# Score packs in two halves, gelu one batch at a time, and new planned durations in a fused attention and GEGLU block

## The chip, the cores and the metric

The kernel runs on one core of a Trainium2 chip. The time is device microseconds from start to end of one execution. Three runs of the kernel before gave a median of 789.99 us (789.24 to 791.8). The engines are TensorE (PE, matmuls), VectorE (DVE), ScalarE (ACT), GpSimd (POOL) and SyncE (SP, which issues most DMAs).

## The reference

One transformer block over 2048 positions of width 640, in bfloat16: layer norm, attention with 32 query heads of width 20 that share one key and one value head, a residual sum, layer norm, and a feed-forward of width 1536 with a gelu gate.

```python
q = (ln(x) @ wq)  # 32 heads of 20
k = ln(x) @ wk;  v = ln(x) @ wv          # one head of 20, shared
p = softmax(q k^T * 20 ** -0.5)
h = x + (p v) @ wo
out = h + (gelu(ln(h) @ w_gate) * (ln(h) @ w_up)) @ w_down
```

## The kernel before

**The work and its tiles.** The 2048 positions are 16 tiles of 128. Attention goes through them in chunks (`CHUNKS`): seven of two tiles and two of one tile, 14 and 15. A chunk is worked in units; a unit is 512 query columns for each of four row strips of the array, so there are 32 units. For each unit and each of 16 key tiles there is one *pack*: four score products of 32 rows by 512 columns, one in each row strip, into four PSUM banks (L1126). That is 512 packs, 2048 products. Each product is then exponentiated into SBUF and multiplied with the values (L1205), accumulating into bank 6 or 7.

**Two ways to the exponential.** ScalarE takes one bank (512 columns) or two adjacent ones (1024) in one activation (L1466). VectorE takes a bank by writing the exponential as a linear function of the bits (L1552); such a product needs two shifted copies, made by GpSimd (L1529, L1515) or VectorE (L1509), and so three value products instead of one. How many of a pack's four products go to VectorE (0, 1, 2, or 4) is decided in `issue_qk` from the planned loads of both engines, the length of the pending shifts, and `stall`, an estimate of ScalarE's wait for the next pack.

**Side products.** Between packs TensorE does everything else in pieces: queries, keys and values, the output projection (`wo_job`), and the feed-forward's gate, up and down products (`gate_job`, `up_job`, `down_job`), all through the helper at L529 (four column strips) while packs are left, or L525 (the whole array) at the end. The feed-forward runs in batches equal to the chunks: 0 to 6 of two tiles, 7 and 8 of one. A batch needs its chunk's attention, the projection and the second layer norm. Its gate products are copied to `gbuf` while exponentials are left (L843), and the gelu is then taken in place on ScalarE (L870); once no exponentials are left, the gelu reads PSUM directly (L845). Exponential and gelu need different activation tables, so each excursion costs a table load both ways. `MERGE` says which batches wait for each other before their gelu: (0,1), (2,3), (4,5), (6,7), (8). Up products follow a batch's gelu, down products its up products, and a later batch may write its part of `gbuf` only when the earlier batch in the same columns is down.

**Who sets the order.** The program holds its own planner. It simulates the five engines with a table of costs (`c_pe`, `c_act`, `c_dve`, L-constants) and picks for the engine that is free first what it does next: `pe_decide`, `act_decide`, `dve_decide`, `pool_decide`, `sp_decide`. `pe_decide` issues a pack when four banks are free, else a value round or a side product that fits before the next pack, else, if TensorE has been quiet, a fill. The result is a fixed list of instructions for each engine, with semaphore waits only where a dependency needs one. On the chip each engine goes through its list in order, as fast as the waits allow. The planner's durations thus set order, not time.

**Other names the change touches.** `LNT`: from this tile on, the second layer norm goes ahead of other VectorE work. `load`: the first DMAs, with the latency that the planner books for each. `xn2T`: the transposed input of the feed-forward; batch b uses columns from 512 times (b mod 2), and may be written when batch b-2 has done its up products. `SP2G`: the gain in ns above which a pack gives VectorE two products.

The condition for a pack, before:

```python
        ok, allb = free_banks(t)
        if cand and len(ok) >= 4:
            issue_qk(t, cand[0], cand[1], ok)
            return True
```

Of the kernel before, what the change touches and what calls it, by code (L numbers as in the profile page):

```python
# [5 lines left out]
BF16 = mybir.dt.bfloat16  # L6
# [3 lines left out]
P = 128  # L10
# [11 lines left out]
class _Op:  # L22
    __slots__ = ("eng", "fn", "deps", "t0", "end", "vis", "idx", "dma", "need", "count", "sem", "clock")

    def __init__(self, eng, fn, deps, t0, end, vis, dma):
        self.eng = eng
        self.fn = fn
        self.deps = deps
        self.t0 = t0
        self.end = end  # L30
        self.vis = vis
        self.dma = dma
        self.need = False
        self.count = 0
        self.sem = None
        self.clock = None


class _Plan:
# [60 lines left out]
    def resolve(self):  # L100
# [6 lines left out]
        while left:  # L107
            moved = False
            for e in self.ENGINES:
                while pos[e] < len(self.ops[e]):  # L110
# [34 lines left out]
                    moved = True  # L145
            assert moved, "the plan has a cycle"
        for e in self.ENGINES:
            n = 0
            for op in self.ops[e]:
                if op.need and not op.dma:  # L150
                    n += 1
                    op.count = n

    def emit(self, name, eng, sems):
        done = 0
        for op, waits in zip(self.ops[name], self.waits[name]):
            for d in waits:
                if d.dma:
                    eng.wait_ge(d.sem, 16)
# [45 lines left out]
def bass_sequential_preLN__grouped_kv_mqa__glu_gated_geglu__prompt_kernel(  # L205
# [29 lines left out]

    CHUNKS = [[0, 1], [2, 3], [4, 5], [6, 7], [8, 9], [10, 11], [12, 13], [14], [15]]
    BATCHES = CHUNKS
    BATCH_COL = [0, 256, 0, 256, 0, 256, 0, 256, 384]
    LN2G = CHUNKS
    MERGE = [(0, 1), (2, 3), (4, 5), (6, 7), (8,)]  # L240
    PE_T1 = (0, 1)
# [5 lines left out]
    ND = 8  # L247
    NQ = 4
    NXT = 4
    NON = 8  # L250
# [10 lines left out]
    xn1T = sb("xn1T", [P, NC_D, S], BF16)  # L261
    xn2T = sb("xn2T", [P, NC_D, 1024], BF16)
    wq_pad = sb("wq_pad", [P, NG, NC_D, P], BF16)
# [6 lines left out]
    wd_sb = sb("wd_sb", [P, NFC, D], BF16)  # L270
    qT = sb("qT", [P, NQ, 512], BF16)
    kT4 = sb("kT4", [P, S], BF16)
    v_ext = sb("v_ext", [P, NT, 3, 32], BF16)
# [6 lines left out]
    onT = sb("onT", [P, 4, NC_D, P], BF16)  # L280
    gbuf = sb("gbuf", [P, NFC, 512], BF16)
    ident = sb("ident", [P, P], BF16)
# [48 lines left out]
    SP2 = 1  # L331
    SP2D = 400.0
    SP2P = 3
    SP2G = 300.0
    ADD_MIN = 1
    PVF = 99
    QUIET = 0.5
    PADD_DVE = 1
    PADD_LEN = 2
    PRA = 3  # L340
# [6 lines left out]
    NP0 = 4  # L347
    LNT = 12
    SPK = 1
# [44 lines left out]
    sp_tasks = []  # L394
    state = {"mode": "m", "tab": "exp", "npack": 0, "exps_left": 2048, "misc_ready": False, "kv_left": NT, "qk_left": 512}
    bank_owner = {b: None for b in range(8)}
    slots = {"xt": list(range(NXT)), "q": list(range(NQ)), "onT": list(range(4)), "osb": [0, 1], "rcp": [0, 1], "onr": [0, 1]}
    pa_free = [True] * NA
# [25 lines left out]
    def ln_group(ln, tiles, prio, done):  # L424
# [27 lines left out]
        def norm(t):  # L452
# [9 lines left out]
            def then(op):  # L462
# [47 lines left out]
    for t in range(NT):  # L510
        on_before[t] = [x for x in range(t) if onslot[x] == onslot[t]]
    xcol = {}
    for b, tl in enumerate(BATCHES):
        for i, t in enumerate(tl):
            xcol[t] = (b % 2) * 512 + i * P

# [95 lines left out]
    def q_job(u):  # L612
# [10 lines left out]
        def then(b):  # L623
# [5 lines left out]
            flex_copy(qT[:, s, :], bank(b), 512, [("b", b)], [("q", s)], 0.6, fin)  # L629

        def gate():
            if u["q"] is None:
# [9 lines left out]
        jb = _Job(("q", u["id"]), 1.0, pieces, then, gate)  # L642
        jobs.append(jb)

# [146 lines left out]
    def g_free(b):  # L791
        if any(("wqp", g) not in plan.w for g in range(NG)):
            return False

        mine = set(gkeys(b, 0))
        return all(down_left[x] == 0 for x in range(b) if mine & set(gkeys(x, 0)))

# [248 lines left out]
    def stall(t, n, fb):  # L1046
# [20 lines left out]
        free.sort()  # L1067
        return max(0.0, free[3] + 460.0 - ta)

    def issue_qk(t, u, kt, fb):  # L1070
        A = max(act_end() - t, 0.0)
        Dv = dve_load(t)
        if state["tab"] == "gelu" or any(tk.engs[0] == "act" for tk in tasks):
            A += sum(tk.cost[1] for tk in tasks if tk.engs[0] == "act" and isinstance(tk.cost, tuple)) + 1300.0
        nf = pd_free.count(True) - len(dve_q)
        burst = A > 3000.0
        if state["npack"] < NP0:
            n = 0
        elif burst:
            n = 4 if Dv < 2500.0 else 2  # L1080
        elif Dv > TH0:
            n = 0
        elif Dv < TH2 or (SP2 and Dv < SP2D and len(pend[1]) + len(pend[2]) < 2 * SP2P
                          and stall(t, 1, fb) + 1382.0 - stall(t, 2, fb) - 956.0 > SP2G):
            n = 2
        else:
            n = 1
        n = max(0, min(n, nf))

        k = state["npack"]  # L1090
        rr = [(k + i) % 4 for i in range(4)]
        bk = {}
        tiles = {}
        want = (4 - n) // 2 if n != 2 or PAIR2 else 0
        fb = list(fb)
# [9 lines left out]
        fb.sort(key=lambda b: ((b ^ 1) in fb, b))  # L1105
        ns = 4 - n - 2 * len(units_a)
        dbanks = [fb.pop(0) for _ in range(n)]
# [30 lines left out]
        for e in al:  # L1138
            act_q.append(("S" if len(e) == 1 else "P", [tiles[r] for r, b in e]))
        u["npk"] += 1  # L1140
        u["left"].remove(kt)
        u["todo"] += 4 + 2 * n
        if not u["left"]:
            u["closed"] = True
            slots["q"].append(u["q"])
        state["npack"] += 1
        _DEBUG.setdefault("joblog", []).append((t, ("qk", u["id"])))
        state["qk_left"] -= 1
# [29 lines left out]
    def issue_pv(t, qs, k):  # L1178
# [69 lines left out]
    def pe_decide(t):  # L1248
        cand = next_pack(t)
        piece = next_piece(t)  # L1250
        state["misc_ready"] = piece is not None
        ok, allb = free_banks(t)
        if cand and len(ok) >= 4:
            issue_qk(t, cand[0], cand[1], ok)
            return True

        tq = 1e12
        if cand:
# [34 lines left out]
        swv = pe_sw(t, "v")  # L1293
        can_v = nr >= 1 and (fits(220.0 + swv) or press)
        can_m = piece is not None and fits(c_pe(piece[1][1], "v") + (
# [23 lines left out]
    def fill(t):  # L1319
# [13 lines left out]
        state["mode"] = "v"  # L1333
        plan.commit("pe", fn, 222.0 + sw, L_PE, ["zz"] + [("k", k) for k in range(4)], [("b", ab)], at=t)
        state["fills"] = state.get("fills", 0) + 1
        return True

    def next_piece(t):
# [26 lines left out]
        for jb in jobs:  # L1365
            pr = jb.prio
            if jb.name[0] == "q":
                ahead = jb.name[1] - cur
                pr = 0.2 if ahead <= 0 else (0.9 if ahead <= 1 else 8.0 + 0.01 * ahead)
            if best is not None and pr >= best[0]:  # L1370
                continue
# [19 lines left out]
    def issue_piece(t, jb, pc):  # L1391
        if isinstance(jb, _Start):
            b = jb.b
            jb = jb.jb
            jobs.remove(jb)
            active.append(jb)
            jb.bank = b
            bank_owner[b] = jb.name
            if jb.name[0] == "q":
                units[jb.name[1]]["q"] = slots["q"].pop(0)  # L1400
        b = jb.bank
        fn = pc[0]
# [133 lines left out]
    def dve_decide(t):  # L1536
# [54 lines left out]
        if n and pend[w][0]["at"] <= t + 20:  # L1591
# [3 lines left out]
            if n >= 4 or pd_free.count(True) < 3:  # L1595
                pr = 0.2
            if n >= (PADD_LEN if POOL_ADD else ADD_MIN):
                opts.append((pr, len(opts), None))
# [109 lines left out]
    sems = {e: sem("c_" + e) for e in plan.ENGINES}  # L1708
    n = 0
    for e in plan.ENGINES:  # L1710
        for op in plan.ops[e]:
            if op.dma:
                op.sem = sem("d%d" % n)
                n += 1
    outs = [op for op in plan.ops["sp"] if op.dma]

    with nc.Block() as block:

        @block.sync
        def _(e):  # L1720
            plan.emit("sp", e, sems)
            for op in outs[-NT:]:
                e.wait_ge(op.sem, 16)

# [48 lines left out]
```

## Time and profile before

| | us |
|---|---|
| median of 3 runs | 789.99 |
| the profiled execution, time | 789.72 |
| its span, first to last instruction | 787.5 |
| PE busy | 688.1 (87%) |
| ACT busy | 728.2 (92%) |
| DVE busy | 622.6 (79%) |
| POOL busy | 626.9 (80%) |

Rows of groups read: line, engine, operation, output from input with shapes, count, then busy us and mean ns of one, then idle time of the engine just before, with what ended it. Rows of the order of time read: start us, length us, what, count; one row may hold several instructions. Rows of windows read: from and to, length, busy us of the engines with the count of instructions in brackets, then the granted TensorE clock, the busy share of the DMA engines and GB/s. A wait row reads: who waited for whom, us in total, times, the longest. A record of an activation or a matmul is longer than the time until the next can start, so records on one engine overlap.

### The profile page before, as it was taken

To read this page: it belongs to the slowest core of one execution; us is meant where nothing else is said; L and a number is where in the kernel's file an instruction comes from. 1 tells how busy PE (TensorE), PEld (TensorE's weight loads), DVE (VectorE), ACT (ScalarE), POOL (GpSimd) and SP (SyncE) were. 2 spreads that over 40 slices of the span, in tenths; PEclk is the share of its full clock that TensorE was granted. 3 is DMA by queue.
4 is the path that set the end of the run, shared out by engine and by line. 5 is a ranking of instruction groups with operands and counts; after the bars stand their busy time and mean duration, and the time that the engine had idled before them with its cause. 6 is when DMAs were issued, how large, how long until landed. Compare 5 with 4: busy or idle time off the path is not lost.

```text
span 787.5 us, 28823 instructions
## 1 busy us (share of the span) xinstructions
PE 688.1 (87%) x12613; PEld 327.8 (42%) x12613; DVE 622.6 (79%) x1128; ACT 728.2 (92%) x1054; POOL 626.9 (80%) x683
## 2 busy tenths in 40 slices
PE   4878778887879899899789899999888889999898
PEld 3322223342334444455234444445233444444477
DVE  7768879878888777977897877877798877877752
ACT  5789999999999999999999999999999999999940
POOL 5579998789978888698978897798998879787810
PEclk9799999999999999999999999999999999999999
DMA  7690000100110002100210001100001010111000
GB/s 204 158 283 12 9 7 19 26 10 8 25 25 9 3 26 27 26 26 10 23 27 2 9 18 34 26 26 10 9 19 26 9 10 26 23 30 26 11 2 34
DMA packets 56604, 25.81 MB, mean 33 GB/s; under 512 B 47649, under 2 KB 55201, under 8 KB 56481
## 3 DMA queue, kind: packets, MB, share of 16 engines
q1 hardware_dynamic: 55168, 23.55, 13.1%
q8 instruction: 100, 1.64, 0.9%
q10 hardware_dynamic: 1312, 0.44, 0.2%
q14 instruction: 24, 0.19, 0.1%
HBM read 10.21 MB, written 2.62 MB: 16 GB/s over the span
## 4 chain that ended last, share of the span: by engine, by line
PE 49%; ACT 30%; DVE 15%; DMA 2%; issue 2%; POOL 2%; POOLq 0%
ACT pa L1466 28%; PE ps L529 18%; PE ps L1126 13%; PE ps L1205 13%; DVE pd L1552 9%; PE ps L525 4%; ACT gbuf L870 1%; DVE xn_tmp L491 1%; DVE osb L1232 1%; DMA onr<-osb 1%; POOL pd L1529 1%; DMA xn1T<-xn_tmp 1%; DVE pd L1509 1%; DMA onT<-onq 1%; DVE gbuf L887 1%
## 5 line engine op out<-in xcount | busy, mean ns | idle before, releaser
L1466 ACT ACTIVATE pa<-ps 128x1024 bf16<-128x1024 f32 (+1 forms) x1013 | 689.0, 836 | 21.1 <-PE ps L1126 15.8
L1529 POOL TENSOR_TENSOR pd<-pd,shifts 128x512 int32<-128x512 int32 x531 | 544.8, 1041 | 94.6 <-DVE pd L1552 88.5
L1552 DVE TENSOR_SCALAR pd<-ps 128x512 uint16<-128x512 f32 x608 | 408.4, 688 | 127.9 <-PE ps L1126 117.1
L1205 PE MATMUL ps<-pd,v_ext 128*32 128x512 bf16 x1824 | 279.8, 384 | 18.1 <-DVE osb L1232 10.2
L1205 PE MATMUL ps<-pa,v_ext 128*32 128x512 bf16 x1440 | 256.7, 385 | 3.1 <-ACT pa L1466 2.5
L1126 PE MATMUL ps<-qT,kT 32*128 32x512 bf16 x2048 | 203.7, 385 | 60.9 <-DVE pd L1552 34.7
L1126 PEld LDWEIGHTS ps<-qT,kT 32*128 32x128 bf16 x2048 | 58.6, 91 | 221.9 <-DVE pd L1552 124.2
L1205 PEld LDWEIGHTS ps<-pd,v_ext 128*32 128x32 bf16 x1824 | 76.8, 95 | 81.2 <-issue 34.7
L1205 PEld LDWEIGHTS ps<-pa,v_ext 128*32 128x32 bf16 x1440 | 68.3, 95 | 39.2 <-issue 24.2
L529 PE MATMUL ps<-xn2T,wg_sb 128*32 128x256 bf16 (+1 forms) x1828 | 68.5, 270 | 1.0 <-DVE gbuf L843 0.5
L529 PE MATMUL ps<-wd_sb,gbuf 128*32 128x320 bf16 x1152 | 57.7, 301 | 1.0 <-DVE gbuf L887 1.0
L529 PE MATMUL ps<-xn2T,wu_sb 128*32 128x256 bf16 x1440 | 58.1, 274 | 0.3 <-DVE gbuf L887 0.3
L529 PE MATMUL ps<-xn1T,wq_pad 128*32 128x256 bf16 (+1 forms) x1440 | 53.3, 272 | 0.5 <-ACT pa L1466 0.4
L529 PEld LDWEIGHTS ps<-xn2T,wg_sb 128*32 128x32 bf16 x1828 | 43.9, 96 | 20.6 <-issue 12.2
L529 PEld LDWEIGHTS ps<-xn2T,wu_sb 128*32 128x32 bf16 x1440 | 36.8, 96 | 16.3 <-issue 7.9
L1515 POOL TENSOR_TENSOR pd<-pd,shifts 128x256 int32<-128x256 int32 x63 | 41.6, 669 | 1.3 <-DVE pd L1552 1.3
L529 PEld LDWEIGHTS ps<-xn1T,wq_pad 128*32 128x32 bf16 x1440 | 34.5, 99 | 16.0 <-issue 8.4
L529 PEld LDWEIGHTS ps<-wd_sb,gbuf 128*32 128x32 bf16 x1152 | 29.0, 96 | 23.3 <-issue 11.1
L887 DVE TENSOR_TENSOR gbuf<-ps,gbuf 128x512 bf16<-128x512 f32 x48 | 32.7, 681 | 6.6 <-PE ps L525 6.1
L1509 DVE TENSOR_SCALAR pd<-pd 128x512 uint16<-128x512 uint16 (+1 forms) x70 | 36.5, 534 | 0.0
L421 DVE BATCH_NORM_STATS2 stats<-xh 128x6 f32<-128x320 bf16 x64 | 29.8, 476 | 1.2 <-DMA xh<-in_A_x_dram 1.0
L529 PE MATMUL ps<-wo_sb,onT 128*32 128x320 bf16 x600 | 28.9, 301 | 1.3 <-DMA onT<-onq 0.7
(73 smaller groups left out, 363.2 us busy)
## 6 DMA issues: line engine op xcount, KB each, us to landing
out_dram<-xh SPq DMA_DIRECT2D x16, 160.0 KB, 1.8
xh<-in_A_x_dram SPq DMA_DIRECT2D x3, 640.0 KB, 8.0
wg_sb<-in_B_w_gate_dram SPq DMA_DIRECT2D x1, 1920.0 KB, 9.7
wu_sb<-in_B_w_up_dram SPq DMA_DIRECT2D x1, 1920.0 KB, 8.3
wd_sb<-in_B_w_down_dram SPq DMA_DIRECT2D x1, 1920.0 KB, 14.0
wo_sb<-in_A_wo_dram SPq DMA_DIRECT2D x1, 800.0 KB, 5.3
onr<-osb SPq DMA_TRANSPOSE x30, 2.4
gbuf<-in_A_wq_dram ACTq DMA_DIRECT2D x1, 400.0 KB, 4.9
```

Of the source, the lines that this page charges most:

```text
L421: dve(lambda e: e.bn_stats(stats[:, ln, t, 6 * h:6 * h + 6], xh[:, t, h * HALF:(h + 1) * HALF]), 395, [key], [("st", ln, t, h)], prio, c)
L491: tk.fn = lambda e: e.tensor_scalar(xn_tmp[:, s, :], xh[:, t, :], mv[:, ln, t, 0:1], ln_r[:, ln, t:t + 1], ALU.subtract, ALU.mult)
L525: return e.matmul(o(b), l, r, start=st, stop=sp)
L529: ins = e.matmul(o(b)[a, :], l[:, a], r, start=st, stop=sp, tile_position=(0, 32 * j))
L887: dve(lambda e: e.tensor_tensor(o, i, o, ALU.mult), c_dve(n * k), [("b", bk)] + ks, ks, 1.0, fin)
L1126: ins = e.matmul(bank(b), kT4[32 * r:32 * r + 32, kt * P:(kt + 1) * P], qT[32 * r:32 * r + 32, s, :], start=True, stop=True, tile_position ...
L1205: ins = e.matmul(ps[32 * r:32 * r + 32, ab * 512:(ab + 1) * 512], v_ext[:, it["kt"], it["w"], :], it["ap"], start=st, stop=(j in ends), ti ...
L1466: op = plan.commit("act", lambda e: e.activation(dst, src, ACT.Exp, scale=SM_SCALE), cost, L_ACT, [("b", b0 + i) for i in range(n)], [("pa ...
L1509: return e.tensor_scalar(pd[:, w, a], pd[:, 0, a], float(CH_SHIFT[w]), None, ALU.add)
L1515: return e.tensor_tensor(pd32[:, w, h], pd32[:, 0, h], shifts[:, w - 1:w].to_broadcast([P, 256 * k]), ALU.add)
L1529: return e.tensor_tensor(pd32[:, 1:3, h], pd32[:, 0, h].unsqueeze(1).to_broadcast([P, 2, 256]), shifts[:].unsqueeze(2).to_broadcast([P, 2, ...
L1552: op = plan.commit("dve", lambda e: e.tensor_scalar(pd[:, 0, s * 512:(s + 1) * 512], bank(b), CH_A, CH_B, ALU.mult, ALU.add), c_dve(512), ...
```

## The change

Several edits in the same program, which is planned anew with all of them:

- A pack may be issued in two halves of two products. When no four banks are free but two are, the side work at hand is at most `LIGHT` = 10 pieces, more than 20 packs are done, ScalarE's table is the exponential's, and ScalarE is planned to wait over 150 ns (`HGAIN`) if the whole pack were waited for, the first two rows are issued; the other two follow when two banks are free. Until then no other pack starts. A half gives VectorE one product if its load is under 1300 ns and fewer than three products wait for shifts, none otherwise (two while ScalarE is away for long).
- `MERGE` splits (4,5) and (6,7) into single batches.
- Planned durations: a side product costs n/2.4 + 3 ns in every mode (before n/2.4 + 9, at least 99, between packs), a value round 216 instead of 222; the value weights' load is booked with 4400 instead of 3000.
- `SP2G` 250 instead of 300; `stall` looks at the third free bank instead of the fourth when little side work is there; `LNT` 8 instead of 12.
- `xn2T` is a ring of four tiles (512 columns instead of 1024); batch 8 now lies beside batch 7 and follows batch 5's columns, not batch 6's. The columns of `gbuf` stay as they were.
- DMAs share semaphores in chains: a DMA joins a chain if the last of it is known to be done when it is issued, and its waiters wait for 16 times its place.
- A way to send queries through memory is added and off (`QD` = 99); `PH` with three equal values each changes nothing.

```diff
-    MERGE = [(0, 1), (2, 3), (4, 5), (6, 7), (8,)]
+    MERGE = [(0, 1), (2, 3), (4,), (5,), (6,), (7,), (8,)]
...
+    HALF_ON = 1
+    HGAIN = 150.0
+    HBEG = 20
+    SIX = 2
+    LIGHT = 10
+    HD0 = 1300.0
+    HP0 = 3
+    QD = 99
...
-        return max(n / 2.4, 54.0) + 3.0 if mode == "m" else max(n / 2.4, 90.0) + 9.0
+        return max(n / 2.4, 26.0) + 3.0
...
-    LNT = 12
+    LNT = 8
...
-    load("sp", wv_sb[:], cview(A_wv), ["wv"], 3000)
+    load("sp", wv_sb[:], cview(A_wv), ["wv"], 4400)
...
-                    return ln == 0 or batch_of[t] < 2 or up_left[batch_of[t] - 2] == 0
+                    return ln == 0 or all(up_left[x] == 0 for x in xshare[batch_of[t]])
...
-        return max(0.0, free[3] + 460.0 - ta)
+        return max(0.0, free[SIX if light(t) else 3] + 460.0 - ta)
...
+    def issue_half(t, u, kt, rows, fb, more):
+
+        A = max(act_end() - t, 0.0)
+        Dv = dve_load(t)
+        nf = pd_free.count(True) - len(dve_q)
+        if A > 3000.0:
+            n = 2
+        elif Dv > TH0:
+            n = 0
+        elif Dv < HD0 and len(pend[1]) + len(pend[2]) < 2 * HP0:
+            n = 1
+        else:
+            n = 0
+        n = max(0, min(n, nf))
+        return issue_rows(t, u, kt, rows, n, fb, more)
+
+    def light(t):
+
+        n = sum(len(j.pieces) - j.pos for j in active)
+        for j in jobs:
+            if all(k in plan.w for k in j.pieces[0][2]) and (j.gate is None or j.gate()):
+                n += len(j.pieces)
+        return n <= LIGHT
...
-        op = plan.commit("pe", fn, 222.0 * k + sw, L_PE, reads, writes, at=t)
+        op = plan.commit("pe", fn, 216.0 * k + sw, L_PE, reads, writes, at=t)
...
-        cand = next_pack(t)
+        half = state["half"]
+        cand = half or next_pack(t)
...
-        if cand and len(ok) >= 4:
+        if half is not None:
+            if len(ok) >= 2:
+                issue_half(t, half[0], half[1], half[2], ok, None)
+                return True
+        elif cand and len(ok) >= 4:
             issue_qk(t, cand[0], cand[1], ok)
             return True
...
+            if half is not None:
+                tq = est[1] if len(est) > 1 else 1e12
+            elif HALF_ON and len(ok) >= 2 and light(t) and tq + 445.0 - act_end() > HGAIN and state["npack"] > HBEG and state[
+                    "tab"] == "exp":
+                k = state["npack"]
+                state["nhalf"] = state.get("nhalf", 0) + 1
+                issue_half(t, cand[0], cand[1], [k % 4, (k + 1) % 4], ok, [(k + 2) % 4, (k + 3) % 4])
+                return True
```

More of the change, by code (lines that the diff above doesn't have):

```diff
@@ L22 @@
 class _Op:
-    __slots__ = ("eng", "fn", "deps", "t0", "end", "vis", "idx", "dma", "need", "count", "sem", "clock")
+    __slots__ = ("eng", "fn", "deps", "t0", "end", "vis", "idx", "dma", "need", "count", "sem", "clock", "chain", "goal")
     def __init__(self, eng, fn, deps, t0, end, vis, dma):
@@ L511, in bass_sequential_preLN__grouped_kv_mqa__glu_gated_geglu__prompt_kernel, with ring @@
         on_before[t] = [x for x in range(t) if onslot[x] == onslot[t]]
+    def ring(sizes, n):
+        at, share, pos = [], [], 0
+        for i, m in enumerate(sizes):
+            if pos + m > n:
+                pos = 0
+            at.append(pos)
+            share.append([j for j in range(i) if at[j] < pos + m and pos < at[j] + sizes[j]])
+            pos += m
+        return at, share
+    xat, xshare = ring([len(b) for b in BATCHES], XR)
+    gat, gshare = ring([len(b) for b in BATCHES], GQ)
+    BATCH_COL = [P * x for x in gat]
     xcol = {}
@@ L640, in gate, with q_load, bind, then @@
             return True
-        jb = _Job(("q", u["id"]), 1.0, pieces, then, gate)
-        jobs.append(jb)
+        if u["id"] >= QD:
+            jobs.append(_Job(("qd", u["id"]), QPRI, pieces, then_far, gate))
+        else:
+            jobs.append(_Job(("q", u["id"]), 1.0, pieces, then, gate))
+    def q_load(u):
+        tk = _Task(("sp",), None, 480, 2000, [("qd", u["id"])], [], 0.1, None)
+        def gate():
+            return bool(slots["q"]) and all(v["q"] is not None for v in units[:u["id"]]) and (
+                u["id"] - cur_unit() <= QAHEAD)
+        def bind():
+            s = slots["q"].pop(0)
+            u["q"] = s
+            tk.writes = [("q", s)]
+            tk.fn = lambda e: e.dma_start(qT[:, s, :], qdr[u["id"]])
+        def then(op):
+            u["qop"] = op
+        tk.gate = gate
+        tk.born = bind
+        tk.then = then
+        sp_tasks.append(tk)
+    def cur_unit():
+        return min([u["id"] for u in units if u["left"]] or [99])
     def normed(u, so, v, key, done):
@@ L793, in g_free @@
             return False
-        mine = set(gkeys(b, 0))
-        return all(down_left[x] == 0 for x in range(b) if mine & set(gkeys(x, 0)))
+        return all(down_left[x] == 0 for x in gshare[b])
     def per_job(b):
@@ L1333, in fill @@
         state["mode"] = "v"
-        plan.commit("pe", fn, 222.0 + sw, L_PE, ["zz"] + [("k", k) for k in range(4)], [("b", ab)], at=t)
+        plan.commit("pe", fn, 216.0 + sw, L_PE, ["zz"] + [("k", k) for k in range(4)], [("b", ab)], at=t)
         state["fills"] = state.get("fills", 0) + 1
```

105 lines of the change are left out of this document (75 added, 30 removed).

## The prediction

> **What bounds the kernel now.** I read the page first (busy shares, slices), then the groups of ScalarE with their forms kept apart, the waits, the chain of waits, and last the order of time around the gelus and at the end. From the page, the busy shares and one row of its forty slices (tenths busy):
>
> ```profile
> PE 688.1 (87%) x12613; PEld 327.8 (42%) x12613; DVE 622.6 (79%) x1128; ACT 728.2 (92%) x1054; POOL 626.9 (80%) x683
> ACT  5789999999999999999999999999999999999940
> ```
>
> ScalarE is full from the third slice to the thirty-eighth and empty in the last two. So there are two stages: about 735 us in which exponentials set the pace, and an end of two slices in which something else does. ScalarE by forms, with columns count, busy us, mean ns and idle before:
>
> ```profile
> L1466 ACT ACTIVATE pa<-ps 128x1024 bf16<-128x1024 f32 x427 | 461.9, 1084 | 3.8 <-PE ps L1126 2.7 <-PE ps L1205 1.0
> L1466 ACT ACTIVATE pa<-ps 128x512 bf16<-128x512 f32 x586 | 365.3, 655 | 17.3 <-PE ps L1126 13.0
> L1466 ACT ACT_TABLE_LOAD x3 | 3.8, 1283 | 0.0
> ```
>
> The same group with its forms together:
>
> ```profile
> L1466 ACT ACTIVATE pa<-ps 128x1024 bf16<-128x1024 f32 (+1 forms) x1013 | 689.0, 836 | 21.1 <-PE ps L1126 15.8
> ```
>
> Records overlap their successors: 461.9 + 365.3 = 827 us singly, 689.0 together. What an exponential costs back to back is seen in an undisturbed stretch of the chain:
>
> ```profile
> 150.26 22.77 ACT pa L1466 x33
> ```
>
> 33 activations there alternate pair and single, so one pair with one single takes 22.77 / 16.5 = 1.38 us, which is the plan's own 904 + 478 ns (L355). At that pace 427 pairs and 586 singles need 666 us. Busy 689.0 and idle 21.1 make 710, so some 44 us of exponential time are waits, half of them hidden inside overlapped records. Who is waited for:
>
> ```profile
> PE ps L1126 <- DVE pd L1552: 34.7, 79, 1.7
> ...
> ACT pa L1466 <- PE ps L1126: 15.8, 32, 1.6
> ```
>
> ScalarE waits for scores, and the score matmul (L1126) waits for VectorE to empty a bank: a pack of four starts only with four free banks.
>
> **Half packs.** The condition asks for few pending side products, so they can only act where no feed-forward runs: about 50–149, 164–233, 367–412 and 547–599 us. Score matmuls there (one for each product; columns: window, length, busy, count):
>
> ```profile
> 50.00:149.00 99.00, 29.34 (x300) 8.59 (x296) 1.00 0.15 42
> 270.00:367.00 97.00, 27.18 (x280) 7.80 (x276) 1.00 0.12 23
> 547.00:599.00 52.00, 15.22 (x156) 4.36 (x152) 1.00 0.12 23
> 610.00:630.00 20.00, 4.04 (x44) 1.18 (x40) 1.00 0.04 9
> ```
>
> The light stretches run at 300/99 = 3.03 and 156/52 = 3.00 products a us, the feed-forward one at 280/97 = 2.89. The four light stretches are 265 us; ScalarE's 44 us of waits spread evenly would put 265/735 of them there, 16 us. A split cannot win more than that, and it can lose. Its price is TensorE time:
>
> ```profile
> 735.78 0.50 PE L529 MATMUL ps<-xn2T,wg_sb 128*32 128x256 bf16 x12
> 736.21 0.40 PE L1126 MATMUL ps<-qT,kT 32*128 32x512 bf16 x4
> 736.53 0.29 PE L529 MATMUL ps<-xn2T,wg_sb 128*32 128x256 bf16 x4
> 736.65 0.38 PE L1205 MATMUL ps<-pa,v_ext 128*32 128x512 bf16 x1
> ```
>
> A side product of 256 columns holds TensorE 0.11 us (736.53 to 736.65, 0.12 rounded), so 512 columns of scores should take 0.21; the next work starts 0.32 after the score pack. So 0.11 goes into the change of array shape, and as much on the way in (three side products, 0.33, from 735.78, yet the pack starts 0.43 later). Two rows of the array take as long as four, so a split adds 0.32 + 0.11 = 0.43 us. The Trainium skill's page TensorEngine Tiling (Array Packing), section Key Properties, says that changing the tiling mode drains TensorE; that speaks against splitting, and the 0.11 us agrees with it; without it a split would add 0.21. In the light stretches TensorE has room:
>
> ```profile
> 100.00:150.00 50.00, 39.63 (x608) 14.99 (x604) 43.16 (x81) 49.18 (x75) 42.85 (x49) 1.00 0.10 20
> ```
>
> 10 us idle in 50 give some 53 us in 265, enough for about 120 splits at 0.43. Between -16 and 0 (a loss is a rival below) I take -5: splits answer only waits over 150 ns, the second half needs two banks again, and GpSimd, 42.85 of 50 busy in this row, must shift each product given to VectorE. The looser bound SP2G (250) and SIX give VectorE a second product more often; the same GpSimd limit makes this part of the -5, not more.
>
> **Gelu, one batch at a time.** Now ScalarE leaves the exponentials once for two batches. The last such event:
>
> ```profile
> 616.10 1.28 ACT L870 ACT_TABLE_LOAD   x1
> 617.39 5.60 ACT L870 ACTIVATE gbuf<-gbuf 128x1536 bf16<-128x1536 bf16 x4
> ```
>
> 8.2 us are gone: a load of 1.29, four gelus in 5.6, and the load back (the row of L1466 above, 1.28). In the window table the 20 us around it had 44 products where 2.89 x 20 = 58 are usual: 14 lost, 4.8 us; so VectorE catches 40%. An event for one batch is 8.2 - 2.8 = 5.4 us long and by the same share costs 3.2. Before: three double events, 14.4 us. After: (0,1), (2,3) double, 4, 5 and 6 single, 9.6 + 9.6 = 19.2. That is +4.8; the ends are +0 (VectorE catches all) and +8 (it catches nothing: four more loads at 1.29 and the two gelus of batch 6 moved in from the end, 2.8). The Trainium skill's page ScalarE: Activation LUTs, section Table sets: the hidden batching unit, says to batch activations by table set, and puts a switch at some 2.66 us with its drain, which speaks against this part. The rows show no drain: the gelu follows 1.29 us after its load starts. By the page's figure the four switches would be 10.6 us of ScalarE, not 5.2, and by the same share the total would be some 3 us later than mine; as the rows show nothing of that drain, it gets no chance of its own.
>
> **What it buys: the end.** From the order of time after the last exponential, TensorE, ScalarE and VectorE in turn:
>
> ```profile
> 756.57 1.52 PE L525 MATMUL ps<-wo_sb,onT 128*128 128x320 bf16 x10
> 757.92 5.62 PE L525 MATMUL ps<-xn2T,wu_sb 128*128 128x256 bf16 x50
> 763.38 0.44 PE L539 MATMUL ps<-ident,xn_tmp 128*128 128x128 bf16 x5
> 763.66 6.68 PE L525 MATMUL ps<-wd_sb,gbuf 128*128 128x320 bf16 x48
> ...
> 776.79 2.40 PE L525 MATMUL ps<-xn2T,wg_sb 128*128 128x128 bf16 x40
> ```
> ```profile
> 750.59 1.28 ACT L845 ACT_TABLE_LOAD   x1
> ...
> 763.86 0.70 ACT L598 ACTIVATE xn2T<-ps 128x640 bf16<-128x640 bf16 x1 [7.08 <-PE ps L539]
> ```
> ```profile
> 754.95 0.48 DVE L599 COPY onT<-ps 128x640 bf16<-128x640 bf16 x1
> ...
> 762.27 0.45 DVE L491 TENSOR_SCALAR xn_tmp<-xh,mv,ln_r 128x640 bf16<-128x640 bf16 x1
> ```
>
> The end is 787.5 - 750.6 = 36.9 us. The 256-column up products and the 48 down products are batch 6 (tiles 12, 13): 5.62 for 50 of its 60 up products, so 6.7 for all, and 6.7 down, 13.4 us. They stand here because batch 6 may not do its gelu before batch 7, whose tile was normalized about 728. Batches 4 and 5 likewise wait for each other; the gate products (wg_sb) and down products (wd_sb) by window:
>
> ```profile
> 500.00:550.00 50.00, 9.01 (x240) 1.00 0.10 22
> 550.00:600.00 50.00, 1.03 (x24) 1.00 0.11 22
> ```
> ```profile
> 700.00:725.00 25.00, 4.88 (x96) 1.00 0.11 28
> ```
>
> and from the chain of waits the second layer norm of tiles 12 and 13, then of tile 14:
>
> ```profile
> 689.83 1.04 DVE ln_veb L437
> ...
> 728.26 1.20 DVE xn_tmp L491
> ```
>
> Batch 4's gate is done before 550 and its gelu comes at 616; the down products of batch 5 reach beyond 700. With single groups batch 4 uses the empty 550–600, batch 5 ends near 660, batch 6 starts its gate when its tiles are ready (near 695) and has 55 us for gate, gelu, up and down. What is left then is the way of tile 15. Its input stands ready at 764.56, 14.0 us after the last exponential; of that 1.1 is its output projection waiting behind TensorE (755.43 to 756.57), 0.7 its transposition (762.72 to 763.38), some 1.2 VectorE's products of batch 6. So 11.0; then a third of its gate (1.1) and the 10.7 us from 776.79 to the end: 22.8 is the floor, 36.9 the ceiling. Tile 14 still has about 10 us of TensorE work, half of which I put into the holes of the first 11 us: 22.8 + 5 = 27.8, so -9.1. The xn2T ring of four lets batch 8 follow batch 5 instead of 6; its transposition is hidden under the same floor, and without that cover would cost the 0.7.
>
> **Head and the rest.** GpSimd in the head:
>
> ```profile
> 6.36 0.27 POOL L941 COPY wk<-wv_sb 128x100 bf16<-128x100 bf16 x1 [2.15 <-DMA wv_sb<-in_A_wv_dram]
> ```
>
> The copy waits 2.15 us for wv, and the first layer norm's power (L441) stands behind it on GpSimd. A load booked at 4400 sends the copy later; I take -1, ends -2.1 and +0.3 (the copy itself now late for the first keys). Shorter product costs (216 for 222; 256 columns 109.7 for 115.7, which the row of 50, 5.62 us, 0.11 each, bears out) change only the order: one side product of 0.11 us more or less ahead of a score pack in some 30 places bounds it at -3 and +3, taken as 0 because TensorE waits for banks. LNT 8 pulls the second layer norm of four tiles ahead, hidden by VectorE's 21% idle, at worst one operation of 0.45 us (row of 762.27) in the way of a score bank for each tile: 0, end +2. Shared DMA semaphores add no wait, since a DMA joins a chain only if its forerunner is known to be done: 0, and at best part of the 2.2 us outside the span. The q scratch is off (QD 99).
>
> **Sum.** -5 + 4.8 - 9.1 - 1 = -10.3 on the profiled 789.72 (span 787.5), so 779.4; the median of the runs, 789.99, is 0.3 above that execution: 779.7.
>
> **Rivals.** *Everything goes well*: batch 7 also finishes inside, the end is 23.5 (-4.3 more), splits win 10 (-5 more): 770. For it: TensorE's idle 10 in 50; against: tile 14 is normalized only near 728. *Splits do nothing* (the waits are VectorE's, and it gets no faster): 785; for it speaks the 34.7 us row, whose releaser is VectorE. *Nothing in sum*: batch 6 leaves its down products and a bit more in the end (end 31.5) and splits do nothing: the gain of 5.4 only pays the events, 789. *TensorE becomes the bound* (the other side): splits and batch 6 draw on the same idle time. 100 splits take 43 us and batch 6 takes 13.4, 56 together; if only 45 of the idle time is usable, the exponential stage grows by 11, splits win nothing: 785 + 11 = 796. It turns slower once under 49 us are usable. Against it: the light stretches alone have 53.
>
> **Chances.** Forecast 0.45; all well 0.19; splits nothing 0.15; nothing in sum 0.07; TensorE bound 0.14. Within 0.3% (2.4 us) counts as the same. Faster 0.79, same 0.07, slower 0.14. The range 769 to 791 leaves out the TensorE case and a little at the lower edge; the forecast's own is 775 to 784.
>
> **What would show it.** Table loads 3 + 3 become 5 + 5; a gelu near 550 and one near 710; the end from the last exponential 26 to 30 us, without 256-column up products; more singles than 586 and fewer pairs; fewer waits of L1126 on VectorE; last exponential near 749. Wrong it would be if batch 6 still stands in the end, or if light stretches run below 3.0 products a us.

## The result and the profile after

The changed kernel takes 791.0 us (median of 6 runs, 789.08 to 795.23), the kernel before 791.84 us in runs on the same chip. The ratio is 1.000, 95% interval 0.9971 to 1.0029: no difference, where 779.7 and a range of 769 to 791 were forecast. Two later executions, of 1030.77 and 1503.83 us, are left out of the medians and ratios below. In what follows the exponential stage runs up to the last exponential, and the end from there to the last instruction. The end did what was forecast. The stage ahead of it grew by as much.

The profiled execution took 791.65 us, span 789.7. Its page, busy shares and the slices of ScalarE:

```profile
PE 697.8 (88%) x12888; PEld 330.4 (42%) x12888; DVE 626.8 (79%) x1144; ACT 730.7 (93%) x1077; POOL 632.6 (80%) x694
...
ACT  5759999999999999999999999999999999999981
```

Three slices differ from before. The last two are 8 and 1 where they were 4 and 0: exponentials run longer and the end is shorter. The third is 5 where it was 8: a hole in the head. ScalarE by forms (L1603 is the exponential now, L953 the gelu in place):

```profile
L1603 ACT ACTIVATE pa<-ps 128x1024 bf16<-128x1024 f32 x396 | 423.8, 1074 | 2.6 <-PE ps L1241 2.2 <-PE ps L1325 0.4
L1603 ACT ACTIVATE pa<-ps 128x512 bf16<-128x512 f32 x635 | 379.3, 656 | 26.7 <-PE ps L1241 22.4 <-PE ps L1325 0.4
...
L953 ACT ACT_TABLE_LOAD x5 | 6.4, 1283 | 0.1
L1603 ACT ACT_TABLE_LOAD x5 | 6.4, 1283 | 0.0
```

Five loads each way where three were, more singles (635 for 586), fewer pairs (396 for 427). At 904 and 478 ns they are 661.5 us of work, 4.6 less than before. Idle before the singles has grown to 26.7 us. The waits say where:

```profile
ACT pa L1603 <- PE ps L1241: 24.5, 42, 8.1
```

One wait alone is 8.1 us long; before, the longest was 1.6. In order of time ScalarE's last exponentials:

```profile
753.72 9.95 ACT L1603 ACTIVATE pa<-ps 128x512 bf16<-128x512 f32 x14 [0.17 <-PE ps L1241]
763.68 1.28 ACT L928 ACT_TABLE_LOAD   x1
```

The end is now 789.7 - 763.7 = 26.0 us, before 36.9: 10.9 gained. The last exponential comes at 763.7 for 750.6: 13.1 lost. By the medians the two kernels are equal, so about 11 of the 13.1 are the change's, and the other 2 lie between these two executions. The question is where the 11 come from.

**The hole in the head.** SyncE's queue (SPq, rows of DMAs as SyncE issues them) of the kernel before, then of the changed one:

```profile
32.29 0.58 SPq L965 DMA_DIRECT2D wo_sb<-in_A_wo_dram  x1
32.91 0.52 SPq L965 DMA_DIRECT2D wg_sb<-in_B_w_gate_dram  x1
36.03 8.59 SPq L482 DMA_TRANSPOSE xn1T<-xn_tmp  x4
44.67 0.58 SPq L965 DMA_DIRECT2D wu_sb<-in_B_w_up_dram  x1
45.29 0.53 SPq L965 DMA_DIRECT2D wd_sb<-in_B_w_down_dram  x1
```
```profile
36.10 0.59 SPq L1048 DMA_DIRECT2D wo_sb<-in_A_wo_dram  x1
36.73 0.53 SPq L1048 DMA_DIRECT2D wg_sb<-in_B_w_gate_dram  x1
37.30 0.53 SPq L1048 DMA_DIRECT2D wu_sb<-in_B_w_up_dram  x1
41.98 7.29 SPq L514 DMA_TRANSPOSE xn1T<-xn_tmp  x2
49.32 0.58 SPq L1048 DMA_DIRECT2D wd_sb<-in_B_w_down_dram  x1
```

In the new order the last two transposes of the layer-normed input, from which the last keys are made, stand behind three weight loads (4.6 MB) and not two (2.7 MB). They take 7.29 us to issue, and the first lands 11.2 us after its issue (median of all 14: 2.7). TensorE waits for them:

```profile
53.81 0.61 PE L575 MATMUL ps<-xn1T,wk 128*32 128x256 bf16 x6 [6.95 <-DMA xn1T<-xn_tmp]
```

Score products up to 60 us, of the kernel before and then of the changed one:

```profile
0.00:60.00 60.00, 10.91 (x100) 2.73 (x100) 0.89 0.76 212
```
```profile
0.00:60.00 60.00, 8.79 (x80) 2.15 (x80) 0.86 0.81 210
```

100 and 80, so five packs of four are missing. The kernel before does its other 487 packs in the 690 us up to its last exponential, 1.42 us each: 7.1 us are lost here. They are not made up soon: by 100 us it is 204 products for 224. The window of 50 to 60 us, in which TensorE stands until 53.8, has a DMA share of 0.99 and a granted clock of 0.66:

```profile
50.00:60.00 10.00, 5.94 (x73) 2.49 (x73) 3.29 (x6) 3.24 (x6) 2.93 (x5) 0.66 0.99 244
```

No step of the prediction had this: the weight loads are in none of the diff's lines.

### The profile page after: what moved, and what is told of

Read it like the earlier page. It is cut to its first block, busy times and chain, and to the rows that moved or that the text cites. A ratio compares the mean times of both kernels' runs of the same rounds, so it can differ in the third digit from the quotient of the medians.

```text
span 789.7 us, 29442 instructions
## 1 busy us (share of the span) xinstructions
PE 697.8 (88%) x12888; PEld 330.4 (42%) x12888; DVE 626.8 (79%) x1144; ACT 730.7 (93%) x1077; POOL 632.6 (80%) x694
## 4 chain that ended last, share of the span: by engine, by line
PE 48%; ACT 29%; DVE 17%; DMA 4%; issue 1%; POOL 1%; DVEq 0%
ACT pa L1603 24%; PE ps L575 19%; PE ps L1241 13%; PE ps L1325 13%; DVE pd L1689 9%; ACT gbuf L953 3%; PE ps L571 2%; DMA xn1T<-xn_tmp 2%; DMA onr<-osb 1%; DVE osb L1352 1%; DVE xn_tmp L523 1%; DVE qT L645 1%; DVE gbuf L970 1%; ACT L1603 1%; ACT L953 1%
## 5 line engine op out<-in xcount | busy, mean ns | idle before, releaser
L1603 ACT ACTIVATE pa<-ps 128x512 bf16<-128x512 f32 (+1 forms) x1031 | 685.4, 816 | 29.3 <-PE ps L1241 24.5
L1689 DVE TENSOR_SCALAR pd<-ps 128x512 uint16<-128x512 f32 x621 | 413.2, 686 | 117.6 <-PE ps L1241 108.1
L1325 PE MATMUL ps<-pd,v_ext 128*32 128x512 bf16 x1863 | 284.6, 385 | 18.5 <-DVE osb L1352 10.2
L1241 PE MATMUL ps<-qT,kT 32*128 32x512 bf16 x2048 | 217.6, 386 | 43.1 <-DVE pd L1689 22.4
L575 PE MATMUL ps<-xn2T,wu_sb 128*32 128x256 bf16 x1680 | 64.5, 274 | 2.8 <-DVE gbuf L970 2.6
L575 PE MATMUL ps<-wd_sb,gbuf 128*32 128x320 bf16 x1344 | 63.4, 301 | 0.6 <-DVE xh L988 0.5
L1652 POOL TENSOR_TENSOR pd<-pd,shifts 128x256 int32<-128x256 int32 x74 | 49.1, 677 | 5.4 <-DVE pd L1689 5.4
L575 PEld LDWEIGHTS ps<-xn2T,wu_sb 128*32 128x32 bf16 x1680 | 42.4, 96 | 20.1 <-issue 9.3
L575 PEld LDWEIGHTS ps<-xn2T,wg_sb 128*32 128x32 bf16 x1808 | 42.3, 96 | 17.7 <-issue 10.9
L575 PEld LDWEIGHTS ps<-wd_sb,gbuf 128*32 128x32 bf16 x1344 | 33.4, 96 | 23.9 <-issue 11.1
L1646 DVE TENSOR_SCALAR pd<-pd 128x512 uint16<-128x512 uint16 (+2 forms) x74 | 39.0, 539 | 0.0
L453 DVE BATCH_NORM_STATS2 stats<-xh 128x6 f32<-128x320 bf16 x64 | 30.1, 478 | 1.6 <-DMA xh<-in_A_x_dram 1.1
## 6 DMA issues: line engine op xcount, KB each, us to landing
wu_sb<-in_B_w_up_dram SPq DMA_DIRECT2D x1, 1920.0 KB, 15.1
```

What stands on the lines that cost most here:

```text
L453: dve(lambda e: e.bn_stats(stats[:, ln, t, 6 * h:6 * h + 6], xh[:, t, h * HALF:(h + 1) * HALF]), 395, [key], [("st", ln, t, h)], prio, c)
L575: ins = e.matmul(o(b)[a, :], l[:, a], r, start=st, stop=sp, tile_position=(0, 32 * j))
L1241: ins = e.matmul(bank(b), kT4[32 * r:32 * r + 32, kt * P:(kt + 1) * P], qT[32 * r:32 * r + 32, s, :], start=True, stop=True, tile_position ...
L1325: ins = e.matmul(ps[32 * r:32 * r + 32, ab * 512:(ab + 1) * 512], v_ext[:, it["kt"], it["w"], :], it["ap"], start=st, stop=(j in ends), ti ...
L1603: op = plan.commit("act", lambda e: e.activation(dst, src, ACT.Exp, scale=SM_SCALE), cost, L_ACT, [("b", b0 + i) for i in range(n)], [("pa ...
L1646: return e.tensor_scalar(pd[:, w, a], pd[:, 0, a], float(CH_SHIFT[w]), None, ALU.add)
```

## The experiments

All ratios are to the kernel before, in runs that share a chip, with 95% intervals.

**First: what the head costs, what the gelus bring, what the halves bring.** *Weights later.* In the changed kernel (`kv_left` counts the tiles whose keys and values are still to be made):

```diff
-   [], [nm], 9.0, None, lambda: plan.free["sp"] > 30000.0))
+   [], [nm], 9.0, None, lambda: plan.free["sp"] > 30000.0 and state["kv_left"] == 0))
```

> The changed kernel with the four weight loads held back until all keys are made; only the order of the SyncE queue differs, every other engine has the same list. Theory (the gain of the end was given back in the head, where the last two key transposes wait behind three weight loads): the 8.1 us wait of ScalarE before 60 us goes, the last exponential comes near 755.5, the time is 783 to 784. Rival (the head's wait is made up later, and the exponential stage is longer for another reason, the gelus or the halves): the wait goes, the time stays within 2 us of 791.

793.76 us, ratio 1.0026 (1.0008 to 1.0044). No gain; if anything a loss. The hole had not gone, it had moved. SyncE, and VectorE behind it:

```profile
44.30 0.58 SPq L1048 DMA_DIRECT2D wo_sb<-in_A_wo_dram  x1
...
46.09 1.13 SPq L1048 DMA_DIRECT2D wd_sb<-in_B_w_down_dram  x1
56.65 3.50 SPq L790 DMA_TRANSPOSE onr<-osb  x1
```
```profile
66.47 0.25 DVE L744 RECIPROCAL rcp<-onr 128x16 f32<-128x16 bf16 x1 [6.64 <-DMA onr<-osb]
```

All four loads, 6.6 MB, now go out together at 44 to 47 us, and the first transpose of an attention result (onr), issued at 56.65, comes after them. VectorE waits 6.64 us in order for it, no bank is emptied, and ScalarE's longest wait is 6.5 us. So the expected 783 was wrong, but so was its rival, which had the wait gone.

*The same edit in the kernel before.*

> The kernel before with the same edit. There two weight loads stand ahead of the last four key transposes and TensorE waits 1.3 us for them. Theory: -1 to -2 us, so the head explains a difference between the two kernels of about 6. Rival (a load near the transposes costs both kernels the same): as much as in the changed kernel, -7.

796.34, ratio 1.0063 (1.0040 to 1.0087): slower. Neither expectation had that. Its loads had stood in two pairs with four transposes between them; held back into one block, they make the same hole there, and ScalarE's longest wait grows from 1.6 to 5.0 us:

```profile
ACT pa L1466 <- PE ps L1126: 21.4, 37, 5.0
```

*Single gelus in the kernel before.*

```diff
-    MERGE = [(0, 1), (2, 3), (4, 5), (6, 7), (8,)]
+    MERGE = [(0, 1), (2, 3), (4,), (5,), (6,), (7,), (8,)]
```

> The kernel before with only the groups of the gelu changed to single batches from batch 4 on; its head is the same. Theory (the step of the end was right: the end 36.9 becomes 26 to 28, two events more cost 4.8): 784 to 786. Rival (each event costs its whole length): the exponential stage grows by 8 to 11 and the time stays at 788 to 791.

788.15, ratio 0.9956 (0.9939 to 0.9972): 3.5 us faster. Its last exponential and its own forms:

```profile
734.30 27.58 ACT L1466 ACTIVATE pa<-ps 128x1024 bf16<-128x1024 f32 x39
761.90 1.28 ACT L845 ACT_TABLE_LOAD   x1
```
```profile
L1466 ACT ACTIVATE pa<-ps 128x1024 bf16<-128x1024 f32 x429 | 463.2, 1083 | 2.1 <-PE ps L1126 1.6 <-PE ps L1205 0.5
L1466 ACT ACTIVATE pa<-ps 128x512 bf16<-128x512 f32 x582 | 362.6, 653 | 20.4 <-PE ps L1126 15.5 <-PE ps L1205 0.3
```

The end is 788.2 - 761.9 = 26.3, 10.6 shorter. The exponential stage is 11.3 longer in this execution, and by the ratio 10.6 - 3.5 = 7.1 (5.8 to 8.4). Four more loads (5.2) and batch 6's gelus moved in from the end (2.8) are 8.0. They pass whole, or nearly: 429 pairs and 582 singles are 666.0 us of exponentials, as the 427 and 586 before; over the whole kernel VectorE has taken nothing off ScalarE. The expectation's range was missed by 2 us, and its rival was right about the events.

*No halves, weights later.* `HALF_ON = 0`.

> The changed kernel with the weight loads held back and no half packs; all else as changed. Theory of the prediction: the halves are worth 5 us, so this is 788 where the one with halves is 783. Rival (43 packs of 512 are split and the score waits on VectorE stay): within 2 us of the one with halves.

793.72, ratio 1.0023 (1.0007 to 1.0040), beside 793.76 with halves. Nothing, as the rival had it. But the hole weighs on this pair: ScalarE's longest wait is 7.7 us without halves and 6.5 with them, so the pair is tried again below without it.

**Second: the loads apart.** If a transpose waits for whatever weights are in flight, the loads must stand apart, each right behind a transpose and far ahead of the next.

```diff
-   lambda: plan.free["sp"] > 30000.0))
+   (lambda t0: lambda: plan.free["sp"] > t0 and state["kv_left"] == 0)(
+       {"wo": 52000.0, "wg": 52000.0, "wu": 70000.0, "wd": 92000.0}[nm])))
```

> The changed kernel with the weight loads behind all key transposes and also apart from each other: two right behind the first attention transpose (onr), one behind the second, one behind the third. Only the order of the SyncE queue differs. Theory (any transpose issued behind several MB of weights waits for them; holding the weights back only moved the wait from the keys to the first onr): no wait over 2 us before 75 us, last exponential near 755, time 7 us under the changed kernel, 784. Rival (the head costs what it costs): as the changed kernel, 791.

786.82, ratio 0.9931 (0.9907 to 0.9955). The list of every other engine is the changed kernel's. SyncE, ScalarE's waits and its last exponential:

```profile
56.88 1.19 SPq L790 DMA_TRANSPOSE onr<-osb  x1
58.11 0.58 SPq L1048 DMA_DIRECT2D wo_sb<-in_A_wo_dram  x1
58.73 0.53 SPq L1048 DMA_DIRECT2D wg_sb<-in_B_w_gate_dram  x1
73.98 1.21 SPq L790 DMA_TRANSPOSE onr<-osb  x1
```
```profile
ACT pa L1603 <- PE ps L1241: 19.2, 43, 1.8
```
```profile
759.17 1.28 ACT L928 ACT_TABLE_LOAD   x1
```

The 8.1 us wait is gone, the stage ends 4.5 us earlier. By the ratios it is 5.5 us, of 7 expected. This settles the hole: the instructions are the same on all engines, and only the loads stand elsewhere.

> The kernel before with the same spread of the loads. Theory: its head waits only 1.3 us for its transposes, so -1 to -2. Rival (the loads cost both kernels the same): -7.

791.38, ratio 0.9996 (0.9971 to 1.0020). The kernel before gains nothing from it that shows in an interval of 2 us either way, so its head was hardly held up. In three runs the transpose lands just behind the last of the weights issued ahead of it (landing: start of the issue plus the time to landing). In the kernel before wg lands at 42.6 us (32.9 + 9.7) and the transpose issued at 36.0 at 43.1. In the changed kernel wu lands at 52.4 (37.3 + 15.1) and the transpose at 53.2, and with the loads held back wd at 66.0 (46.1 + 19.9) and the onr at 66.5. The rows agree with the Trainium skill's page DMA: Bandwidth & Descriptors, section Two DMAs through the same engine are not ordered, which says that within one queue of a DMA engine descriptors start in order. The landings speak for the order of the queue; that it alone does it, and not the load on the engines, no run here separates.

> The changed kernel with spread loads and no half packs. The prediction's 5 us for the halves: 5 us over the one with halves. Rival (43 splits of about 150 to 400 ns waits are worth what the two runs with held loads showed, nothing): within 1.5 us of it.

783.99, ratio 0.9906 (0.9873 to 0.9938), the fastest kernel of the study: 7 us under the changed one, 8 under the kernel before on its own chip. The interval overlaps that with halves (0.9931), so a loss through halves is not shown; a gain of 5 us is excluded, the most that the two intervals allow is some 2.5 us. What the halves do shows in the forms, first without and then with them, weights spread in both:

```profile
L1603 ACT ACTIVATE pa<-ps 128x1024 bf16<-128x1024 f32 x411 | 435.6, 1064 | 2.3 <-PE ps L1241 2.3
L1603 ACT ACTIVATE pa<-ps 128x512 bf16<-128x512 f32 x597 | 361.8, 639 | 22.9 <-PE ps L1241 15.7 <-PE ps L1325 1.5
```
```profile
L1603 ACT ACTIVATE pa<-ps 128x1024 bf16<-128x1024 f32 x396 | 421.8, 1069 | 3.3 <-PE ps L1241 2.8 <-PE ps L1325 0.4
L1603 ACT ACTIVATE pa<-ps 128x512 bf16<-128x512 f32 x635 | 377.5, 648 | 20.9 <-PE ps L1241 16.4 <-PE ps L1325 0.4
```

and in the waits of the score products, in the same order:

```profile
PE ps L1241 <- DVE pd L1689: 34.8, 82, 1.0
```
```profile
PE ps L1241 <- DVE pd L1689: 24.0, 57, 1.1
```

The planner makes 43 splits. They do what they are for: the scores' waits on VectorE's banks fall from 34.8 to 24.0 us. ScalarE gets next to nothing from it. 411 pairs and 597 singles are 656.9 us of work, 396 and 635 are 661.5: 8 products have gone back from VectorE to ScalarE and pairs have become singles, 4.6 us more for the engine that sets the pace, and its idle time before exponentials falls by only 1.0, to 24.2 from 25.2.

> The changed kernel with spread loads and the old groups of the gelu, (4,5) and (6,7). By the prediction's terms (end -9.1, events +4.8) 4.3 us slower than the single ones; by the run of the old kernel with single gelus, where the end won 11 and the exponential stage lost 8 to 11, 3 to 4 us slower. Rival (events and end cancel): within 1.5 us.

791.56, ratio 1.0000 (0.9979 to 1.0022), against 0.9931 with single groups: single gelus are worth 5.5 us here. In this kernel the planner put the third group inside the stage and the fourth late in it; the last exponentials are these:

```profile
749.87 1.28 ACT L953 ACT_TABLE_LOAD   x1
...
756.69 2.98 ACT L1603 ACTIVATE pa<-ps 128x512 bf16<-128x512 f32 x5
```

Its stage ends at 759.7 and its end is 792.5 - 759.7 = 32.8, for 759.2 and 26.0 with single groups: the difference lies in the end.

**Third: the other edits.** *The booked latency of wv undone alone.* `["wv"], 3000` in the changed kernel, loads as changed.

> The changed kernel with the value weights' load booked at 3000 again, nothing else undone. In its list three key transposes, not two, follow one or two weight loads, as in the kernel before. Theory (the booked latency moved the planner's order in the head, and with it the loads): the wait of 8 us before 60 us goes, 784 to 787. Rival (another edit set that order): the wait stays, 791.

790.69, ratio 0.9984 (0.9967 to 1.0001): not told from the changed kernel. The 8.1 us wait is 3.4 here,

```profile
49.83 1.57 ACT L1603 ACTIVATE pa<-ps 128x512 bf16<-128x512 f32 x2 [3.42 <-PE ps L1241]
```

and 88 score products are done by 60 us, where the changed kernel has 80 and the kernel before 100. So this edit had a part in the order of the head, but the hole is not gone. What undoing it gives back, the new plan that comes with it takes at the end:

```profile
735.26 27.72 ACT L1603 ACTIVATE pa<-ps 128x512 bf16<-128x512 f32 x41
```

The last exponential ends at 763.0 and the end is 793.1 - 763.0 = 30.1 us, where the changed kernel has 26.0. Which edits together made the order stays open.

*The old planned costs*, with loads spread and no halves:

```diff
-        return max(n / 2.4, 26.0) + 3.0
+        return max(n / 2.4, 54.0) + 3.0 if mode == "m" else max(n / 2.4, 90.0) + 9.0
...
-        op = plan.commit("pe", fn, 216.0 * k + sw, L_PE, reads, writes, at=t)
+        op = plan.commit("pe", fn, 222.0 * k + sw, L_PE, reads, writes, at=t)
...
-        can_v = nr >= 1 and (fits(216.0 + swv) or press)
+        can_v = nr >= 1 and (fits(220.0 + swv) or press)
...
-        plan.commit("pe", fn, 216.0 + sw, L_PE, ["zz"] + [("k", k) for k in range(4)], [("b", ab)], at=t)
+        plan.commit("pe", fn, 222.0 + sw, L_PE, ["zz"] + [("k", k) for k in range(4)], [("b", ab)], at=t)
```

> Spread loads, no halves, and the old planned costs of side products and value rounds (all else changed). The prediction put the costs at 0, so 784 as the run without halves. Rival (TensorE's order with the true costs is worth something, the plan itself books 7 us): 787 to 791.

789.47, ratio 0.9968 (0.9945 to 0.9990), against 0.9906 (0.9873 to 0.9938) with the new costs: 5 us slower, the intervals just apart. The rival was right that the costs matter; the prediction had 0. ScalarE's forms and its last exponentials:

```profile
L1603 ACT ACTIVATE pa<-ps 128x1024 bf16<-128x1024 f32 x418 | 449.5, 1079 | 1.3 <-PE ps L1241 1.2
L1603 ACT ACTIVATE pa<-ps 128x512 bf16<-128x512 f32 x594 | 367.1, 650 | 20.1 <-PE ps L1241 14.1
```
```profile
752.00 2.92 ACT L1603 ACTIVATE pa<-ps 128x512 bf16<-128x512 f32 x4 [0.15 <-PE ps L1241]
```

418 pairs and 594 singles are 661.8 us, 4.9 more than the 656.9 with the new costs, yet ScalarE waits less (21.4 us for 25.2) and its last exponential ends at 754.9, 1.8 earlier. It is the end that is longer: 786.3 - 754.9 = 31.4 us for 25.6. 87 down products stand in it where 48 do with the new costs. The 39 more are batch 6's, 5.8 us of TensorE. With side products booked too long, the plan leaves them over for the end.

*The old SP2G and the fourth free bank*, loads spread, no halves: `SP2G = (300.0, 300.0, 300.0)`, `SIX = 3`.

> Spread loads, no halves, and SP2G 300 and the fourth free bank in the estimate of the wait, as before (all else changed). The prediction had this in the 5 us of the halves: if more products for VectorE are the part of it that is real, ScalarE's exponentials take 5 to 9 us more (fewer products on VectorE) and the time is 788 to 791. Rival (GpSimd allows no more): within 1.5 us of 784.

788.70, ratio 0.9960 (0.9943 to 0.9976), against 0.9906: 4 us slower. The forms:

```profile
L1603 ACT ACTIVATE pa<-ps 128x1024 bf16<-128x1024 f32 x419 | 445.2, 1068 | 1.1 <-PE ps L1241 1.1
L1603 ACT ACTIVATE pa<-ps 128x512 bf16<-128x512 f32 x591 | 360.4, 644 | 23.2 <-PE ps L1241 18.2 <-PE ps L1325 0.8
```

419 pairs and 591 singles are 661.3 us, 4.4 more than the 656.9 with the looser bound: ten products that VectorE no longer takes. That is the reason that was expected, but it does not show as 4 us of the stage: in this execution the last exponential ends at 757.4, 0.6 later, and the end is 785.3 - 757.4 = 27.9 us, 2.3 longer. How the ten products cost 4 us is not shown.

*The kernel before with spread loads and single gelus.*

> The kernel before with spread loads and single gelus from batch 4 on, nothing else. From the runs so far: single gelus -3.5, spread loads 0, so 788. What lies between this and the 784 of the changed kernel with spread loads and no halves is then due to costs, SP2G with the free bank, LNT and the head's order together: 4.

787.05, ratio 0.9941 (0.9921 to 0.9961), as expected within its interval. That leaves about 3 us between it and the 0.9906 of the changed kernel without halves and with spread loads, and the two intervals overlap. `LNT`, the ring of `xn2T` and the shared semaphores are part of that difference; none of them was undone alone. Costs and bound, taken out one at a time, cost 5 and 4: parts of a replanned schedule do not add up. How much any new plan moves the time, whatever the edit, no run here measures.

## Why the prediction was wrong

The measured 791.0 lies at the upper edge of the range (769 to 791), and the gain that was forecast did not come. The steps that failed are the head, forecast at -1, which cost 5.5 us, and the half packs, forecast at -5, which brought nothing. By its own steps:

- **What bounds the kernel now**: right, ScalarE's pace and then an end of another kind. The half packs' reason, that scores wait for banks of VectorE, was right as well.
- **The end, -9.1**: right in mechanism and nearly in size, -10.9 in the changed kernel and -10.6 with the single gelus alone. Batch 6 leaves the end: no 256-column up products are left in it, and 48 down products where 96 stood.
- **Gelu events, +4.8**: mechanism right, size wrong. What failed in it is that VectorE "catches 40%" of an event and that this share holds. It was read from 20 us around one event. Over the kernel the exponential work is 666 us with three events and with five, so what VectorE took there it gave back elsewhere, where is not shown, and the 8.0 is added whole or nearly. The range of this term had +8 as its end. The net with the end, some 4.3, came out at 3.5 to 5.5.
- **Table switches at 2.66 us**, the figure of the Trainium skill's page ScalarE: Activation LUTs, section What ACT_TABLE_LOAD costs: the loads show 1283 ns, with 0.1 and 0.0 us of idle before them in all, and the gelu follows 1.30 us after the start of its load (565.81 after 564.51 in the changed kernel); no run shows the drain.
- **Half packs, -5**: wrong. The ceiling of 16 us was the time ScalarE waits; the step missed that a half packs other products than a whole: 4.6 us more work for ScalarE against the waits it saves. Measured between nothing and a small loss. The part of that -5 which was real was the looser bound for a second VectorE product, 4 us when taken out alone, which I had counted as no more than a share because of GpSimd.
- **Planned costs, 0**: with the halves out they are worth -5. "Change only the order" was true, but the term was bounded at ±3 by what a side product does to a score pack; what the order decides is how many side products are done before the last exponential, 39 of batch 6's down products in that run.
- **The head, -1**: wrong, and the step that decided. The prediction considered only the new start of the first layer norm (the first exponential comes at 14.1 us for 14.6). The new plan moved everything in the head, the weight loads on SyncE's queue too, which the prediction took as they stood. The planner books a transpose the same time whether or not weights are in flight. It cost 5.5 us by the ratio of the run that undid it (7 in packs by 60 us).

Put together, by the ratios along one path of runs: single gelus and spread loads take 4.7 us off the kernel before, the other edits but the halves 2.8 more, the halves give back 2.0, and the loads where the changed kernel has them another 5.5. The sum is nothing; each step is known to 2 or 3 us. Without the last two steps the kernel gains 7.4 us, where 10.3 were forecast. Of the rivals, the one that the splits do nothing was right in what they bring. Its reason was not, since the waits on VectorE did fall, and its 785 did not have the head. TensorE did not become the bound: where no feed-forward runs the changed kernel does score products as fast as the kernel before, 272 in 60 to 149 us in both (3.06 a us).

## What to carry to other kernels

Where a program plans itself, any edit of a cost or a due time moves everything, so look at every queue of the new order for what now stands behind large transfers, those of untouched lines too, and place bulk loads apart in gaps between the small transfers that a tight loop waits for. A planned duration that is too long also costs time: work that the plan thinks does not fit is left over for the end. A share read from a short stretch around an event is not a share of the whole: check the pacing engine's total work by counts before taking a catch-up for granted. A wait that is shortened is worth something only if the cure gives the pacing engine no more work than the wait was.

## What the runs showed of the hardware that was not expected

A transpose DMA issued behind weights in flight took about three times as long to issue: two key transposes behind 4.6 MB held SyncE 7.29 us, where two with no weights ahead took 2.52 us (the changed kernel with the loads held back):

```profile
41.74 2.52 SPq L514 DMA_TRANSPOSE xn1T<-xn_tmp  x2
```

And the hole left a mark after itself. In the changed kernel TensorE stood from 46.9 to 53.8 us; its granted clock was 1.00 up to 50 us, 0.73 from 50 to 52, 0.50 from 52 to 56, when it was at work again, 0.56 from 56 to 58 and 1.00 from 58 to 60. A record of a score product lasts 0.61 us at 55.89, for 0.39 at 46.47. With the loads spread, where TensorE had work, the clock was 1.00 from 50 to 60. What the clock goes by is not shown: the kernel before has 0.50 from 28 to 36 us, with TensorE at work.
